# Five load tiles instead of three for the experts' weights, three instead of two for 64-bit input

## The chip, the cores and the metric

The kernel runs on one core of one Trainium2 chip. The core has five engines that each work through a queue of their own in order: TensorE (PE in the profile, with its weight loads as PEld), VectorE (DVE), ScalarE (ACT), GpSimd (POOL) and SyncE (SP), which here issues most of the DMAs. The metric is the device time of one execution in microseconds (us).

## What is computed

Three stages follow each other on the same data.

```python
X = np.fft.rfft(x, axis=1); y = np.fft.irfft(X * F, n=S, axis=1)        # (8, 3072, 256)
# mixture of experts on the 24576 rows, 8 experts, room for 768 rows each
h = np.maximum(np.einsum('ecd,edf->ecf', disp, w1), 0.0)                 # w1 (8, 256, 1024)
y = np.einsum('ecf,efd->ecd', h, w2)                                     # w2 (8, 1024, 256)
out[i] = gate_w[i] * y[expert_idx[i], pos[i]]                            # rows without a place stay zero
# then on all rows
return ((x @ w_a) * (x @ w_b)) @ w_out                                   # w_a, w_b (256, 1536), w_out (1536, 256)
```

The three matrices of the last stage arrive as 64-bit numbers.

## The kernel before

The program runs through a Fourier stage (to about 220 us), the experts' stage (to about 545 us) and the stage of the last three matrices (to the end). The change touches the experts' stage and what is done beside it.

**Steps.** The 8 experts have 768 places each, in 2 blocks of 384 rows: 16 blocks. A block is worked in 8 steps, one for each 128 of the 1024 hidden columns; `for s in range(nstep + 2)` counts 128 steps. In step s, `up` (L674) makes the hidden columns of one chunk with 6 matmuls, ACT and DVE split them into a high and a low half (`hh` L682, `hl` L683), and `down` (L686) adds the columns of step s-2 to the result with 6 matmuls. At a block's end ACT copies the result out (`yb`, L695) and stores it (L1155). In the fourth and fifth step of a block the rows of the next block are turned (L657 on PE, `xh` L658 on ACT, `xl` L659 on DVE), and in the seventh POOL fetches those of the block after it with three gathers (L646).

**Weights.** A chunk is 128 hidden columns of one expert, w1 and w2 together, 256 KB: 88 chunks, since experts 0 to 2 are loaded twice (their two blocks don't follow each other: the order is block 0 of experts 0, 1, 2, then block 1 of the same, then both blocks of 3 to 7). `load_chunk` (L618) gives each chunk a load on SP into a tile `raw` (two DMAs, L627 and L628) and a split: ACT copies it to `wh` (L633) and POOL subtracts to get `wl` (L634). The first 10 chunks have tiles of their own. From the 11th on the tiles `raw` are shared, a load waits until POOL has made `wl` of the chunk that had the tile, and a chunk is split in a fixed step, `at`, seven steps before its first use, and loaded in step `at - 3` of the program. While experts change with every block (steps 3 to 50) each step splits a chunk; later 8 of every 16 steps do.

**Conversion.** Beside this the 64-bit matrices are converted, 36 pieces, spread evenly over steps 17 to 119 (`convert`, L516; `moe2_steps`, L555). SP loads a piece into `raw64`; ACT squares its high words (`sq`, L533); DVE makes `ex` and `bits` (L534, L535), and half a piece later finishes (L541 to L544) into a tile `mix`, of which there are two. Two pieces make a factor of `w_a` or `w_b`: POOL makes four sums in `mix` (L579 to L582), ACT copies the high half (L564) and POOL subtracts the low half (L565, 2.1 us), after which `mix` is free. `ex` lies in PSUM, all else in SBUF.

**Zeros.** The rows of the output that no expert writes are filled from a tile of zeros by 48 DMAs on SP (L185), 18 of them in this stage. The tile `wide` holds zeros in its first half and the first rows of `w_out` in its second.

The order on each queue is the order in which the code is written; nothing is rescheduled.

Of the kernel before, what the change touches and what calls it, by code (L numbers as in the profile page):

```python
# [10 lines left out]
F32 = mybir.dt.float32  # L11
F32R = mybir.dt.float32r
# [9 lines left out]
P = 128  # L22
# [105 lines left out]
class Kernel:  # L128
# [48 lines left out]
            for k in range(4):  # L177
                nc.tensor.matmul(p[:, P * k:P * k + P], self.warm, self.warm, start=True, stop=True)

    def zero_steps(self, pool):  # L180

        v = self.io["out"].rearrange("(i p r) d -> i p r d", p=P, r=4)
        z = pool.tile([P, D], F32, name="zero")
        self.nc.vector.memset(z, 0.0)
        steps = [lambda i=i: self.nc.sync.dma_start(out=v[i], in_=bc(z[:, None, :], [P, 4, D]))  # L185
                 for i in range(NT // 512)]
        n = NB0 * S // 512
        return steps[:n], steps[n:]
# [327 lines left out]
    def convert(self, pc, src, to, pp=None):  # L516


        nc = self.nc
        v = nc.vector  # L520
        T = {}

        def load():
            T["raw"] = pc.tile([P, 256], I64, tag="raw64", name="raw64", bufs=2)
            nc.sync.dma_start(T["raw"], src)

        def make():
            w = T["raw"].bitcast(I32).rearrange("p (n t) -> p n t", t=2)
            lo, hi = w[:, :, 0].bitcast(U32), w[:, :, 1]
            ex = T["ex"] = (pp or pc).tile([P, 256], I32, tag="ex", name="ex", bufs=1)  # L530
            bits = T["bits"] = pc.tile([P, 256], I32, tag="bits", name="bits", bufs=1)
            sq = T["sq"] = pc.tile([P, 256], F32, tag="sq", name="sq", bufs=1)
            nc.scalar.activation(sq, hi.bitcast(F32), AF.Square)  # L533
            v.tensor_scalar(ex, hi, 3, 0x3FFFFFF8, ALU.logical_shift_left, ALU.bitwise_and)  # L534
            v.scalar_tensor_tensor(bits, hi, -0x40000000, ex, ALU.bitwise_and, ALU.bitwise_or)  # L535
            T["lo"] = lo

        def finish():
            bits, ex, sq, lo = T["bits"], T["ex"], T["sq"], T["lo"]
            f = ex.bitcast(F32)  # L540
            v.tensor_scalar(ex, bits, -0x800000, None, ALU.bitwise_and)  # L541
            v.scalar_tensor_tensor(f, lo, 2.0 ** -52, ex.bitcast(F32), ALU.mult, ALU.mult)
            v.tensor_tensor(f, f, bits.bitcast(F32), ALU.add)
            v.scalar_tensor_tensor(to(), sq.rearrange("p (a n) -> p a n", a=2), LEAST,  # L544
                                   f.rearrange("p (a n) -> p a n", a=2), ALU.is_ge, ALU.mult)

        return load, make, finish

    def moe2_tiles(self, pw):
        self.W = {n: (pw.tile([P, NU, 7, P], F32R, name=n + "h"), pw.tile([P, NU, 7, P], F32R, name=n + "l"))  # L550
                  for n in ("w_a", "w_b")}
        self.W["wide"] = pw.tile([P, 2 * D], F32R, name="wide")
        self.W["w_out"] = (pw.tile([P, 2 * DFF], F32R, name="w_outh"), pw.tile([P, 2 * DFF], F32R, name="w_outl"))

    def moe2_steps(self, pc, pp=None):  # L555


        nc, io = self.nc, self.io
        g = nc.gpsimd
        work = []  # L560

        def parts(src, dst):
            h, l = dst
            nc.scalar.copy(h, src)  # L564
            g.tensor_tensor(l, src, h.bitcast(F32), ALU.subtract)  # L565

        def factors(n, u):
            T = {}

            def c0():  # L570
                m = T["m"] = pc.tile([P, 8, P], F32, tag="mix", name="mix", bufs=2)
                return m[:, 0:8:7, :]

            def c1():
                return T["m"][:, 1:4:2, :]

            def mix():
                m = T["m"]
                g.tensor_tensor(m[:, 4], m[:, 7], m[:, 3], ALU.add)  # L579
                g.tensor_tensor(m[:, 5], m[:, 4], m[:, 0], ALU.subtract)  # L580
                g.tensor_tensor(m[:, 6], m[:, 0], m[:, 7], ALU.subtract)
                g.tensor_tensor(m[:, 2], m[:, 1], m[:, 5], ALU.subtract)  # L582

            src = io[n].rearrange("(c p) f -> p c f", p=P)[:, :, 256 * u:256 * u + 256]
            work.append(self.convert(pc, src[:, 0, :], c0, pp) + (None, None))
            work.append(self.convert(pc, src[:, 1, :], c1, pp) + (
                mix, lambda: parts(T["m"][:, 0:7, :], [t[:, u] for t in self.W[n]])))

        def plain(f):
            T = {}  # L590

            def to():
                T["o"] = pc.tile([P, 8, P], F32, tag="mix", name="mix", bufs=2)[:, 0:2, :]
                return T["o"]

            work.append(self.convert(pc, io["w_out"].rearrange("(c p) d -> p c d", p=P)[:, f, :], to, pp) + (
                None, lambda: parts(T["o"].rearrange("p a n -> p (a n)"),
                                    [t[:, f * D:f * D + D] for t in self.W["w_out"]])))

        def wide():  # L600
            nc.vector.memset(self.W["wide"][:, 0:D].bitcast(F32), 0.0)
            nc.vector.tensor_copy(self.W["wide"][:, D:], self.W["w_out"][0][:, 0:D].bitcast(F32))

        for u in range(NU):
            for n in ("w_a", "w_b"):
                factors(n, u)
        for f in range(DFF // P):
            plain(f)

        def step(i, stages):  # L610
            for k in stages:
                at = i - (0, 2, 2, 3, 4)[k]
                if 0 <= at < len(work) and work[at][k]:
                    work[at][k]()

        return [lambda i=i, k=k: step(i, k) for i in range(len(work) + 4) for k in ((1, 3), (2, 0, 4))] + [wide]

    def load_chunk(self, pa, e, f, pr=None, eng=None):  # L618
# [4 lines left out]
        T = {}  # L623

        def load():
            raw = T["raw"] = (pr or pa).tile([P, 4, P], F32, tag="raw", name="raw", bufs=NWC if pr else 3)
            nc.sync.dma_start(raw[:, 0:2, :], w1[:, P * f:P * f + P].rearrange("(c p) f -> p c f", p=P))  # L627
            nc.sync.dma_start(raw[:, 2:4, :].rearrange("p c d -> p (c d)"), w2[P * f:P * f + P, :])  # L628

# [40 lines left out]
    def ffn(self, pb, pp, w, x, y):  # L670
# [4 lines left out]
        def up(f):  # L675
            wh, wl = w[f]["h"], w[f]["l"]
            hp = self.ps()
            for c in range(2):
                self.mm3(hp[:, :BLK], wh[:, c, :], wl[:, c, :], x["h"][:, c, :], x["l"][:, c, :], c == 0, c == 1)
            hh = pb.tile([P, BLK], F32R, tag="hh", name="hh", bufs=4)  # L680
            hl = pb.tile([P, BLK], F32R, tag="hl", name="hl", bufs=4)
            nc.scalar.activation(hh, hp[:, :BLK], AF.Relu)  # L682
            nc.vector.scalar_tensor_tensor(hl, hp[:, :BLK], 0.0, hh.bitcast(F32), ALU.max, ALU.subtract)  # L683
            T[f] = (hh, hl)
# [240 lines left out]
def fast_path(K, outer):  # L925
# [4 lines left out]
    with ExitStack() as ctx:  # L930
# [177 lines left out]
        for c in range(NWC, 8 * len(turns)):  # L1108
            o = c - NWC
            at = (start[o // 8 + 1] - 1) * 8 + o % 8 + 3  # L1110
            ch = chunk(c)
            due.setdefault(at - 3, []).append(ch[0])
            due.setdefault(at, []).append(ch[1])
        conv, zero = [], []
        def load(k):
# [15 lines left out]
        for s in range(nstep + 2):  # L1131
# [6 lines left out]
            if s == 8 * NE - 9:  # L1138
# [4 lines left out]
                K.moe2_tiles(pw)  # L1143
                pc = pool("pc", "right", sC)
                conv = K.moe2_steps(pc, pp)
                zero, K.zeros = K.zero_steps(pw)
            if s < nstep:
                ups[k][s % 8]()
            for step in due.get(s, []):
# [143 lines left out]
```

## Time and profile before

| | |
|---|---|
| median of 3 runs | 1135.81 us (1134.91 to 1136.91) |
| profiled execution | 1140.07 us, of which the span of the core 1138.3 us |
| mean granted TensorE clock | 0.982 |
| busy in the span | PE 94%, PEld 90%, DVE 73%, POOL 59%, ACT 39% |

The profiled execution is 4.26 us above the median of the runs that were only timed. Matmuls overlap in the profile (one of 384 columns takes about 0.33 us and the next begins 0.17 us after it), so that a busy PE says less than the distance between the starts of its matmuls. A figure in brackets behind a row of the timeline is how long the engine was idle before it, and what ended that.

### The profile page before, as it was taken

Reading aid. Unit: us, or ns where it says so; the run is one execution under the profiler, and the core shown is the slowest. Engines: PE = TensorE matmul, PEld = TensorE weight load, DVE = VectorE, ACT = ScalarE, POOL = GpSimd, SP = SyncE. Lnnn points to the kernel's source line nnn. Section 1 sums busy time; section 2 is a strip of 40 time slices with the busy share of each in tenths; the row PEclk is TensorE's granted clock in tenths of the full one; section 3 lists DMA queues with packets and bytes.
Section 4 is the critical chain, followed back from the end, with each engine's and each line's share of the span. In section 5 each row is a group of like instructions: output and inputs, shape, how many; then the busy total and the mean of one; then the engine's idle time right before and its main releaser. Section 6 shows DMA issues by size and latency. Waiting matters only on the chain.

```text
span 1138.3 us, 19329 instructions
## 1 busy us (share of the span) xinstructions
PE 1075.0 (94%) x6908; PEld 1027.6 (90%) x6908; DVE 827.7 (73%) x1590; ACT 441.8 (39%) x894; POOL 673.9 (59%) x676
## 2 busy tenths in 40 slices
PE   7799998899998899999999999999999999999993
PEld 6777897869988899999899999999999999999993
DVE  2638788575456666673778888888888888888873
ACT  3564543454555555554332232332323223232220
POOL 1412645566788787653364765757657576575752
PEclk9999998989999999999999999999999999999997
DMA  9965824433667655662404004040040000100000
GB/s 222 192 210 178 258 71 140 122 133 127 196 221 216 200 175 180 205 201 78 153 1 138 30 1 149 20 139 29 1 149 20 29 28 1 38 19 1 29 1 31
DMA packets 109097, 123.27 MB, mean 108 GB/s; under 512 B 8576, under 2 KB 92544, under 8 KB 108992
## 3 DMA queue, kind: packets, MB, share of 16 engines
q1 hardware_dynamic: 93152, 87.34, 26.4%
q10 hardware_dynamic: 11232, 22.02, 5.3%
q0 software_dynamic: 4608, 12.59, 3.5%
q8 instruction: 56, 0.92, 0.3%
q14 instruction: 49, 0.40, 0.1%
HBM read 68.44 MB, written 53.48 MB: 107 GB/s over the span
## 4 chain that ended last, share of the span: by engine, by line
PE 72%; DMA 7%; issue 6%; POOL 5%; DVE 5%; SPq 2%; ACT 1%; POOLq 0%; DVEq 0%; ACTq 0%
PE ps L666 12%; PE ps L667 12%; PE ps L668 11%; PE po L831 6%; PE po L830 6%; PE po L829 5%; DMA raw<-w 3%; PE ps L374 3%; PE ps L333 3%; PE ps L310 3%; PE yp L667 2%; PE yp L668 2%; PE yp L666 2%; PE ps L391 2%; POOL wl L634 2%
## 5 line engine op out<-in xcount | busy, mean ns | idle before, releaser
L758 POOL TENSOR_TENSOR gl<-w_b,gh 128x384 fp32r<-128x384 f32 x190 | 194.3, 1034 | 196.0 <-ACT gh L757 195.8
L757 ACT CAST gh<-w_b 128x384 fp32r<-128x384 f32 x192 | 98.7, 514 | 262.2 <-DVE w_b L776 196.9
L830 PE MATMUL po<-w_outl,gh 128*128 128x256 f32 x576 | 160.9, 279 | 0.0
L831 PE MATMUL po<-w_outh,gl 128*128 128x256 f32 x576 | 160.6, 279 | 0.2 <-POOL gl L758 0.2
L829 PE MATMUL po<-w_outh,gh 128*128 128x256 f32 x552 | 154.0, 279 | 0.0
L634 POOL TENSOR_TENSOR wl<-raw,wh 128x512 fp32r<-128x512 f32 x88 | 112.6, 1291 | 52.9 <-ACT wh L633 30.1
L324 POOL TENSOR_TENSOR y<-t,t 112x512 f32<-112x512 f32 x48 | 65.7, 1368 | 129.8 <-DVE t L323 100.0
L683 DVE SCALAR_TENSOR_TENSOR hl<-ps,hh 128x384 fp32r<-128x384 f32 x128 | 70.5, 554 | 78.9 <-ACT hh L682 76.5
L666 PE MATMUL ps<-th,w_bh 128*128 128x384 f32 x336 | 114.7, 341 | 4.4 <-DVE w_a L769 4.4
L666 PE MATMUL ps<-th,w_ah 128*128 128x384 f32 x336 | 113.5, 338 | 1.2 <-DVE w_b L769 0.8
L667 PE MATMUL ps<-tl,w_ah 128*128 128x384 f32 x336 | 113.6, 338 | 1.1 <-DVE tl L723 0.5
L668 PE MATMUL ps<-th,w_al 128*128 128x384 f32 x336 | 113.2, 337 | 0.0
L667 PE MATMUL ps<-tl,w_bh 128*128 128x384 f32 x336 | 113.2, 337 | 0.0
L668 PE MATMUL ps<-th,w_bl 128*128 128x384 f32 x336 | 113.1, 337 | 0.0
L831 PEld LDWEIGHTS po<-w_outh,gl 128*128 128x128 f32 x576 | 108.1, 188 | 1.5 <-POOL gl L758 0.4
L830 PEld LDWEIGHTS po<-w_outl,gh 128*128 128x128 f32 x576 | 108.0, 187 | 0.0
L829 PEld LDWEIGHTS po<-w_outh,gh 128*128 128x128 f32 x552 | 103.6, 188 | 0.0
L666 PE MATMUL ps<-xh,wh 128*128 128x384 f32 x256 | 91.8, 359 | 5.8 <-DVE hl L683 5.2
L790 ACT COPY p<-ps 128x384 f32<-128x384 f32 x96 | 46.0, 479 | 127.4 <-PE ps L668 69.6
L776 POOL TENSOR_TENSOR w_b<-w_b,w_a 128x384 f32<-128x384 f32 x94 | 93.8, 1019 | 0.0
L682 ACT ACTIVATE hh<-ps 128x384 fp32r<-128x384 f32 x128 | 62.5, 488 | 74.1 <-PE ps L668 66.8
L666 PE MATMUL yp<-hh,wh 128*128 128x384 f32 x256 | 86.4, 337 | 4.9 <-ACT yb L695 4.7
(158 smaller groups left out, 2811.1 us busy)
## 6 DMA issues: line engine op xcount, KB each, us to landing
out<-zero SPq DMA_DIRECT2D x48, 512.0 KB
raw<-w SPq DMA_DIRECT2D x176, 128.0 KB
rows<-yt ACTq DMA_DIRECT2D x18, 512.0 KB
da<-sa ACTq DMA_DIRECT2D x12, 512.0 KB
sb<-da SPq DMA_DIRECT2D x32, 192.0 KB
yd<-yb ACTq DMA_DIRECT2D x16, 384.0 KB
y<-yd SPq DMA_DIRECT2D x8, 768.0 KB
sd<-x SPq DMA_DIRECT2D x12, 256.0 KB
```

The costliest lines, as they stand in the source:

```text
L324: eng.tensor_tensor(y, t1, t2, ALU.add)
L634: (eng or nc.gpsimd).tensor_tensor(l, T["raw"], h.bitcast(F32), ALU.subtract)
L666: mm(out, wh, xh, start=first, stop=False)
L667: mm(out, wh, xl, start=False, stop=False)
L668: mm(out, wl, xh, start=False, stop=last)
L683: nc.vector.scalar_tensor_tensor(hl, hp[:, :BLK], 0.0, hh.bitcast(F32), ALU.max, ALU.subtract)
L757: nc.scalar.copy(gh, g)
L758: (v if hurry and not ij[1] else nc.gpsimd).tensor_tensor(gl, g, gh.bitcast(F32), ALU.subtract)
L776: (v if hurry or ij in ON_V else nc.gpsimd).tensor_tensor(c, c, T["a"][ij], ALU.mult)
L829: mm(out, gh[:, sl], oh[:, o:o + D], start=False, stop=False)
L830: mm(out, gh[:, sl], ol[:, o:o + D], start=False, stop=False)
L831: mm(out, gl[:, sl], oh[:, o:o + D], start=False, stop=u == NU - 1 and i == 1 and j == 0)
```

## The change

`raw` gets five tiles and the loads stand one step earlier in the program; `raw64` gets three. Room is made in four places: `sq` moves from SBUF to PSUM, into one tile `two` with `ex`; the finishing steps leave their sum in `bits` (SBUF), where `ex` (PSUM) had it; `hh` and `hl` have three tiles each, not four; and the zeros are read from `wide`, whose first half is now cleared when the tile is made, so that the tile `zero` goes.

```diff
@@ zero_steps
-        z = pool.tile([P, D], F32, name="zero")
-        self.nc.vector.memset(z, 0.0)
+        z = wide[:, 0:D].bitcast(F32)
@@ convert
-            T["raw"] = pc.tile([P, 256], I64, tag="raw64", name="raw64", bufs=2)
+            T["raw"] = pc.tile([P, 256], I64, tag="raw64", name="raw64", bufs=3)
...
-            ex = T["ex"] = (pp or pc).tile([P, 256], I32, tag="ex", name="ex", bufs=1)
+            two = (pp or pc).tile([P, 2, 256], I32, tag="two", name="two", bufs=1)
+            ex, sq = T["ex"], T["sq"] = two[:, 0], two[:, 1].bitcast(F32)
             bits = T["bits"] = pc.tile([P, 256], I32, tag="bits", name="bits", bufs=1)
-            sq = T["sq"] = pc.tile([P, 256], F32, tag="sq", name="sq", bufs=1)
...
-            f = ex.bitcast(F32)
+            f = bits.bitcast(F32)
             v.tensor_scalar(ex, bits, -0x800000, None, ALU.bitwise_and)
-            v.scalar_tensor_tensor(f, lo, 2.0 ** -52, ex.bitcast(F32), ALU.mult, ALU.mult)
-            v.tensor_tensor(f, f, bits.bitcast(F32), ALU.add)
+            v.scalar_tensor_tensor(ex.bitcast(F32), lo, 2.0 ** -52, ex.bitcast(F32), ALU.mult, ALU.mult)
+            v.tensor_tensor(f, ex.bitcast(F32), f, ALU.add)
@@ moe2_tiles
         self.W["wide"] = pw.tile([P, 2 * D], F32R, name="wide")
+        self.nc.vector.memset(self.W["wide"][:, 0:D].bitcast(F32), 0.0)
@@ moe2_steps, wide
-            nc.vector.memset(self.W["wide"][:, 0:D].bitcast(F32), 0.0)
@@ load_chunk
-            raw = T["raw"] = (pr or pa).tile([P, 4, P], F32, tag="raw", name="raw", bufs=NWC if pr else 3)
+            raw = T["raw"] = (pr or pa).tile([P, 4, P], F32, tag="raw", name="raw", bufs=NWC if pr else 5)
@@ ffn, up
-            hh = pb.tile([P, BLK], F32R, tag="hh", name="hh", bufs=4)
-            hl = pb.tile([P, BLK], F32R, tag="hl", name="hl", bufs=4)
+            hh = pb.tile([P, BLK], F32R, tag="hh", name="hh", bufs=3)
+            hl = pb.tile([P, BLK], F32R, tag="hl", name="hl", bufs=3)
@@ fast_path
-            due.setdefault(at - 3, []).append(ch[0])
+            due.setdefault(max(0, at - 4), []).append(ch[0])
             due.setdefault(at, []).append(ch[1])
```

The order of the instructions on PE and POOL is the same in both programs. On SP the loads of weights move past the loads of 64-bit input and the zeros. This is SP's queue about step 22 before (the numbers are those of the program's tiles; `raw_3057` is one chunk's tile, `raw64_3039` one piece's):

```order
L525 DMA raw64_3039<-w_b 128x256 [waits DMAHW5_49,DVE_49]
L627 DMA raw_3057<-w1 128x2x128 [waits DMAHW6_49,DMAHW7_49,DMAHW0_49,Pool_49]
L628 DMA raw_3057<-w2 128x256
L627 DMA raw_3087<-w1 128x2x128 [waits DMAHW2_49,DMAHW1_49,Pool_49]
L628 DMA raw_3087<-w2 128x256
L525 DMA raw64_3103<-w_b 128x256 [waits DMAHW3_49,DVE_49]
L185 DMA out<-zero_2775 512x1x256 [waits DMAHW4_49]
L627 DMA raw_3121<-w1 128x2x128 [waits DMAHW5_49,Pool_49]
```

And the same place on SP in the changed program:

```order
L524 DMA raw64_3040<-w_b 128x256 [waits DMAHW7_49]
L627 DMA raw_3058<-w1 128x2x128 [waits DMAHW0_49,Pool_49]
L628 DMA raw_3058<-w2 128x256 [waits DMAHW1_49]
L627 DMA raw_3087<-w1 128x2x128 [waits DMAHW2_49,Pool_49]
L628 DMA raw_3087<-w2 128x256 [waits DMAHW3_49]
L524 DMA raw64_3103<-w_b 128x256 [waits DMAHW4_49,DVE_49]
L184 DMA out<-wide_2772 512x1x256 [waits DMAHW5_49]
L627 DMA raw_3121<-w1 128x2x128 [waits DMAHW7_49,Pool_49]
```

The sequence looks alike there, but each load of weights now stands one step ahead of the step that it belonged to, and its wait for POOL is for the subtraction of the chunk five before it in place of three; the second DMA of a chunk has got a wait for an earlier DMA on its semaphore (DMAHW).

On DVE the conversion of one piece, between the splits of the hidden columns (`hl`) and of turned rows (`xl`), stood like this before:

```order
L534 TENSOR_SCALAR ex<-raw_3039 128x256 [waits DMAHW5_49,DVE_49]
L535 SCALAR_TENSOR_TENSOR bits<-raw_3039,ex 128x256 [waits DVE_49]
L683 SCALAR_TENSOR_TENSOR hl<-ps,hh 128x384 [waits Activation_49]
L659 TENSOR_TENSOR xl<-ps,xh 128x384 [waits Activation_49]
L541 TENSOR_SCALAR ex<-bits 128x256 [waits DVE_49]
```

In the changed program the same five rows on DVE are:

```order
L534 TENSOR_SCALAR two<-raw_3040 128x256 [waits DMAHW7_49,Activation_49]
L535 SCALAR_TENSOR_TENSOR bits<-raw_3040,two 128x256 [waits DVE_49]
L683 SCALAR_TENSOR_TENSOR hl<-ps,hh 128x384 [waits Activation_49]
L659 TENSOR_TENSOR xl<-ps,xh 128x384 [waits Activation_49]
L541 TENSOR_SCALAR two<-bits 128x256 [waits DVE_49]
```

The first of them has got a wait for ACT: for the square of the same piece, which now writes into the same tile of PSUM.

On ACT, at the end of a block, copies and store stood like this before:

```order
L633 CAST wh<-raw 128x512 [waits DMAHW7_49,DMAHW6_49]
L695 COPY yb<-yp 128x384 [waits PE_49] x2
L1155 DMA yd_2008<-yb 128x768 [waits Activation_49]
L682 ACTIVATE hh<-ps 128x384 [waits PE_49]
L633 CAST wh<-raw 128x512 [waits DMAHW2_49,DMAHW1_49]
```

In the changed program this place on ACT reads:

```order
L633 CAST wh<-raw 128x512 [waits DMAHW7_49,DMAHW6_49]
L695 COPY yb<-yp 128x384 [waits PE_49] x2
L1155 DMA yd_2008<-yb 128x768 [waits DMAHW4_49,Activation_49]
L682 ACTIVATE hh<-ps 128x384 [waits DVE_49,PE_49]
L633 CAST wh<-raw 128x512 [waits DMAHW1_49,DMAHW0_49]
```

The store of a block's result has got a wait for an earlier DMA, here one of the loads of weights that were issued a few steps before, and `hh` one for DVE's reading of the tile's former content.

## Rows read from the trace of the kernel before

**Rows 1.** Page, 40 slices of the span, busy tenths of PE and POOL.
```profile
PE   7799998899998899999999999999999999999993
POOL 1412645566788787653364765757657576575752
```

**Rows 2.** Stretches: us, busy time of each engine, granted clock, DMA share, GB/s.
```profile
301.30:383.37 82.07, 72.92 (x410) 68.85 (x410) 49.32 (x115) 45.12 (x95) 69.94 (x71) 1.00 0.67 210
340.00:360.00 20.00, 16.98 (x97) 16.10 (x97) 12.64 (x30) 11.62 (x25) 19.07 (x21) 1.00 0.69 211
383.37:400.68 17.31, 17.31 (x104) 17.24 (x103) 13.83 (x34) 10.40 (x21) 11.57 (x13) 1.00 0.74 229
```

**Rows 3.** Timeline of PE: first matmul of steps 23, 55, 63, 71, 79 and 87.
```profile
301.30 0.33 PE L666 MATMUL ps<-xh,wh 128*128 128x384 f32 x1
...
383.37 0.33 PE L666 MATMUL ps<-xh,wh 128*128 128x384 f32 x1
...
400.68 0.33 PE L666 MATMUL ps<-xh,wh 128*128 128x384 f32 x1
...
419.82 0.33 PE L666 MATMUL ps<-xh,wh 128*128 128x384 f32 x1
...
437.14 0.33 PE L666 MATMUL ps<-xh,wh 128*128 128x384 f32 x1
...
455.27 0.33 PE L666 MATMUL ps<-xh,wh 128*128 128x384 f32 x1
```

**Rows 4.** Waits from 301.30 to 383.37: us in total, times, longest us.
```profile
ACT wh L633 <- DMA raw<-w: 30.7, 18, 5.0
DVE hl L683 <- ACT hh L682: 23.1, 11, 4.2
POOL wl L634 <- ACT wh L633: 9.7, 9, 2.0
...
DVE mix L544 <- POOL w_bl L565: 2.8, 1, 2.8
```

**Rows 5.** Waits of SP's DMA queue from 283 to 384 us.
```profile
SPq L627 <- POOL wl L634: 35.5, 23, 5.0
...
SPq L525 <- DVE ex L542: 7.1, 2, 3.7
```

**Rows 6.** Timeline: one weight tile's way through POOL, SP and ACT to PE.
```profile
345.39 1.30 POOL L634 TENSOR_TENSOR wl<-raw,wh 128x512 fp32r<-128x512 f32 x1
346.72 0.38 SPq L627 DMA_DIRECT2D raw<-w  x1
347.14 0.81 SPq L628 DMA_DIRECT2D raw<-w  x1
350.77 0.62 ACT L633 CAST wh<-raw 128x512 fp32r<-128x512 f32 x1 [2.71 <-DMA raw<-w]
351.82 0.45 PE L666 MATMUL yp<-hh,wh 128*128 128x384 f32 x1 [2.79 <-ACT yb L695]
```

**Rows 7.** Timeline of ACT, in the blocks from 400.68 and 437.14.
```profile
413.06 0.62 ACT L633 CAST wh<-raw 128x512 fp32r<-128x512 f32 x1 [3.67 <-DMA raw<-w]
...
449.35 0.63 ACT L633 CAST wh<-raw 128x512 fp32r<-128x512 f32 x1 [3.16 <-DMA raw<-w]
```

**Rows 8.** Groups of POOL from 301.30 to 383.37: busy, mean ns, idle before.
```profile
L646 POOL DMA_INDIRECT rowt<-rows,gidx x12 | 12.0, 1003 | 3.0 <-issue 2.1 <-PE yp L668 0.3
```

**Rows 9.** Timeline of DVE: two finishing instructions that waited for POOL.
```profile
372.11 0.42 DVE L544 SCALAR_TENSOR_TENSOR mix<-sq,ex 128x256 f32<-128x256 f32 x1 [2.79 <-POOL w_bl L565]
...
478.82 0.42 DVE L544 SCALAR_TENSOR_TENSOR mix<-sq,ex 128x256 f32<-128x256 f32 x1 [4.30 <-POOL w_outl L565]
```

**Rows 10.** Timeline of DVE and ACT: first instructions of one 64-bit piece.
```profile
366.54 0.42 DVE L534 TENSOR_SCALAR ex<-raw 128x256 int32<-128x256 int32 x1
...
366.65 0.43 ACT L533 ACTIVATE sq<-raw 128x256 f32<-128x256 f32 x1
```

**Rows 11.** Timeline: clearing of `zero` on DVE, last store of rows on ACT.
```profile
284.21 0.27 DVE L184 MEMSET zero<- 128x256 f32 x1
...
259.96 0.40 ACTq L395 DMA_DIRECT2D rows<-yt  x1
```

More of the change, by code (lines that the diff above doesn't have):

```diff
@@ L178, in warm_up, with zero_steps @@
                 nc.tensor.matmul(p[:, P * k:P * k + P], self.warm, self.warm, start=True, stop=True)
-    def zero_steps(self, pool):
+    def zero_steps(self, wide):
         v = self.io["out"].rearrange("(i p r) d -> i p r d", p=P, r=4)
-        z = pool.tile([P, D], F32, name="zero")
-        self.nc.vector.memset(z, 0.0)
+        z = wide[:, 0:D].bitcast(F32)
         steps = [lambda i=i: self.nc.sync.dma_start(out=v[i], in_=bc(z[:, None, :], [P, 4, D]))
@@ L1145, in fast_path @@
                 conv = K.moe2_steps(pc, pp)
-                zero, K.zeros = K.zero_steps(pw)
+                zero, K.zeros = K.zero_steps(K.W["wide"])
             if s < nstep:
```

## The prediction

> **What bounds the kernel now.** I began with the page's slices [rows 1]: PE is busy at eight or nine tenths almost everywhere, and POOL at seven to eight tenths from the eleventh slice to the sixteenth (a slice is 28.5 us), some 285 to 455 us. In the first part of that stretch each step of the experts' stage splits a chunk, so the two engines are compared there.
>
> The starts of PE's first matmul of a step give the length of each block [rows 3]. The block 383.37 to 400.68 takes 17.31 us, and its stretch shows PE busy for all of it [rows 2]: that is what 8 steps cost when nothing is late. The four blocks from 301.30 to 383.37 take 82.07 us where 4 x 17.31 = 69.24 would do, so **12.83 us** are lost. Later blocks lose less: 400.68 to 419.82 is 19.14 (1.83 lost), 437.14 to 455.27 is 18.13 (0.82 lost). The granted clock is 1.00 in all of these stretches, which is the 2.4 GHz level, so the loss is waiting and not a lower clock.
>
> Next, who waits for what there [rows 4]. The largest line is ACT, 30.7 us in 18 waits of the copy `wh` for `raw`, up to 5.0 each. Second is DVE's `hl` for ACT's `hh`, 23.1 us: a consequence, since `hh` stands behind `wh` in ACT's queue. SP's queue tells why `raw` is late [rows 5]: 23 loads waited 35.5 us for POOL's `wl`. The reader can follow one turn of this circle in the timeline [rows 6]: POOL ends `wl` at 346.69, the load is issued 0.03 us later, its second half at 347.14 for 0.81, ACT starts the copy only at 350.77 after 2.71 us of idling, then copies `yb`, and PE has stood still 2.79 us for that `yb` when it starts at 351.82. ACT's queue is worked in order, so the late copy holds back `yb` though PE has its result ready. The same wait appears once each in the later lossy blocks: 3.67 at 413.06 and 3.16 at 449.35 [rows 7].
>
> So PE pays for a transfer that begins only when POOL has finished. But POOL itself is nearly full. In the four blocks it is busy 69.94 us [rows 2], and its 12 gathers have 3.0 us before them in which it issues [rows 8]: 72.9 us of work it can't avoid, which is more than PE's 69.24. Between 340 and 360 us it is busy 19.07 of 20, with three gathers' issuing (2.1 x 3/12 = 0.5) 98%.
>
> **The change part by part.**
>
> *Five tiles, loads a step earlier.* A load now waits for the `wl` of the chunk five before. Two more chunks are two steps, at least 2 x 17.31/8 = 4.3 us of lead, against waits of 1.7 us on average (30.7/18) and 5.0 at most: nearly every wait of `wh` for `raw` should go. What comes back is not the whole 12.83. ACT and PE can then run ahead only as far as POOL follows: `wl` is still made chunk by chunk, and POOL must do 72.9 us of work. Lower bound of the gain: POOL reaches no more than the 98% that it already shows: 72.9/0.98 = 74.4, gain 82.07 - 74.4 = **7.7**. With POOL never idle it is 9.2; if POOL's work could be caught up in the blocks after it (in 383.37 to 400.68 it is busy only 11.57 of 17.31) and PE never waited, 12.83. I take 7.7, since POOL's row is the nearest to a bound: its split of a chunk is due seven steps ahead, which is some slack, but five tiles still tie loads, and the two `mix` tiles tie DVE, to where POOL stands.
>
> For the later blocks: at 413.06 the load of that chunk waited likewise for a `wl` that stood behind POOL's backlog; with two chunks more the backlog no longer reaches the load, and I count the whole 1.83. For 437.14 to 455.27 I count half, 0.4, because a block with turned rows and 64-bit pieces has other small waits (bounds 0 and 0.82). Other blocks gain nothing: one of them loses 1.9 us to DVE's wait of 4.30 at 478.82 for POOL's `w_outl` [rows 9], which no tile of `raw` touches.
>
> *Three tiles for 64-bit input.* SP's loads of 64-bit pieces waited 7.1 us for DVE between 283 and 384 [rows 5], and a load of weights behind them on the same queue waits with them. With three tiles they wait for the finish of the piece three before, which lies further back. Gain beside the first part: nothing, as loads of weights will be early anyway. Without it, the loads would be held up to 3.7 us, inside the 4.3 us of lead.
>
> *`sq` in PSUM with `ex`.* The number of instructions is the same. DVE's first instruction of a piece now waits for ACT's square. In the trace DVE began it at 366.54, and ACT the square at 366.65 for 0.43 [rows 10]: it would slip about 0.5 us. Behind it in DVE's queue stand the rest of the piece and the next `hl`; but that `hl` waits for `hh`, which stands behind the square on ACT anyway. So the cost is mostly covered: bounds 0 and 36 pieces x 0.5 = 18 us if each slip reached PE. I take 0.01 per piece, about 0.3 us, nearest to the row of `hl`, which waits for ACT 23.1 us in these blocks already.
>
> *`hh` and `hl` with three tiles.* A tile is read by `down` two steps after its making, and PE does that `down` before the next `up`, by program order. So PE can't want a fourth. `hh` now waits for DVE's reading of a tile written three steps ago: over 6 us back. Cost 0; if DVE lagged three steps behind, PE would already stand.
>
> *The store of a block's result* on ACT now also waits for an earlier load on the same semaphore. That load is one that a coming `wh` needs anyway. While loads are early it costs nothing; if late, `hh` behind it waits as it did before. I take 0.2 us over all blocks, bounds 0 and one load's 2.7 [rows 6].
>
> *The zeros from `wide`.* One clearing of 0.27 us on DVE goes and another moves from the conversion to the making of the tile [rows 11]. The clearing must wait for the stores of rows that read the same room; the last was issued at 259.96, 24 us ahead of 284.21. Cost 0, cover 24 us.
>
> **Sum:** 7.7 + 1.8 + 0.4 - 0.3 - 0.2 = **9.4 us**. Nothing after 545 us changes but its start. The profiled execution of 1140.07 would become 1130.7; it lies 4.26 above the median, and that stays, so the median goes from 1135.81 to **1126.4**.
>
> The Trainium skill ("Perfetto Trace Analysis", Identifying the Most-Contended Engine) says to improve the engine with the highest occupancy, and to judge TensorE by its weight loads, not by its matmuls. By that rule POOL is the engine between 340 and 360 (19.07, weight loads 16.10 of 20 [rows 2]), and the change takes no work off it. The trace bears the rule out in so far as every late load begins 0.03 us after POOL's `wl`; by it the four blocks could give at most POOL's idle time, 82.07 - 72.9 = 9.2, where the waits alone would give 12.83.
>
> **The rivals.** A measurement of this kernel tells about 0.2% (2.3 us) from no change.
>
> *A, the forecast:* POOL bounds the four blocks, 6 to 13 us come back, chance 0.62.
>
> *B, the backlog comes out elsewhere.* ACT and DVE no longer held by `raw`, the conversion runs into its two `mix` tiles: DVE's last finishing instruction waits for POOL's part, as it does at 372.11 for 2.79 and at 478.82 for 4.30 [rows 9], and `hl` stands behind it. The four blocks are 32 of the 103 steps over which 36 pieces are spread, so some 11 pieces or 5 to 6 factors fall into them; at 0.5 to 1 us more each, 3 to 6 us of the 9.4 are lost again. Gain 2.3 to 6, about 1132. For it: POOL's rows. Against it: only one such wait is in the four blocks, 2.8 us [rows 4]. Chance 0.18.
>
> *C, no change.* Either the loads are late by the transfer itself (the DMA share is 0.67 there [rows 2], and if more loads in flight only share the same engines, landing slips by as much as issue gains), or POOL's whole backlog eats the gain. Against it: in the undisturbed block the DMA share is higher, 0.74, and nothing waits. Time 1134 to 1138. Chance 0.11.
>
> *D, slower.* The square stands behind a `wh` in ACT's queue; DVE's first instruction waits through that, with `xl` and `hl` behind it. It decides the sign when the 36 pieces cost more than (9.4 + 2.3)/36 = 0.33 us each on PE's path. At the 0.5 us of slip all uncovered it is 18 us against 9.7 gained, 1144. Against it: the cover named above; DVE is busy 49.32 of 82.07 [rows 2]. Chance 0.06.
>
> The Trainium skill ("PSUM — Partial Sum Buffer", PSUM bank collisions raise a hardware error) says that ScalarE and VectorE must be kept from one bank of PSUM at the same time whatever the addresses. The order of the changed program agrees: the new wait stands where `sq` and `ex` share a tile; no run here shows what would happen without it.
>
> *E, more than forecast.* POOL catches up behind the blocks and PE loses nothing: 12.83 + 1.83 + 0.82 = 15.5, so 1120.3. Against it: POOL's 72.9 beside PE's 69.24. Chance 0.03 for more than 13.
>
> **How the numbers follow.** The time is A's. Its own range, 6 to 13 us, is 1122.8 to 1129.8 with chance 0.62; to hold 8 in 10 the range must take in most of B, up to 1132.5 (a gain of 3.3), and below it reaches E's bound, 1120.5. Left out are C, D and the weak end of B, about 0.2. Faster by over 0.2%: A, B and E, 0.83. Same: C, 0.11. Slower: D, 0.06.
>
> **What would show it.** Right: between 301 and 383 the waits of `wh` for `raw` fall from 30.7 to under 5 us; PE's four blocks take 73 to 76 us; POOL is busy over 93% of them; the waits of the SP queue for `wl` may stay, but are no longer followed by an idle ACT; the idling at 413.06 and 449.35 is gone; a block without splits still takes 17.31. B shows as longer waits of `mix` L544 for POOL's parts and of `hl` behind them; C as `wh` waiting for `raw` as before with loads issued earlier; D as waits of `two` L534 for ACT, with PE waiting for `hl`. The prediction is wrong if the four blocks take over 79 or under 70 us, or if the time moves outside the experts' stage.

## The result and the profile after

The changed kernel takes **1126.36 us** (median of 5 runs, 1124.34 to 1128.39), before 1135.81 in the same comparison: ratio 0.9918, 95% interval 0.9897 to 0.9939. That is faster by more than the 0.2% named in the prediction.

The two profiled executions differ by more, 1138.3 and 1122.5 us of span, and this has to be cleared up first. From the first matmul of step 7 (260.41 before, 253.97 after) to that of step 127 (543.22 and 527.40) the change saves 282.81 - 273.43 = **9.38 us**; behind step 127 both spans have 595.1 us left. The other 6.4 us lie ahead of step 7, where the granted clock between 210 and 240 us was 0.90 in the one execution and 1.00 in the other. In the twelve experiments step 0 began between 225.1 and 231.1 us, and steps 0 to 7 took between 25.2 and 29.9 us, whatever was changed, so these 6.4 us are taken as the execution's, not the kernel's. From here on kernels are compared over steps 7 to 127. Each kernel has one profiled execution, so a difference of a microsecond or so between two stretches is a hint and no more.

PE's first matmuls of steps 23, 31, 39, 47 and 55 in the timeline of the changed kernel (start, duration) answer to [rows 3]:

```profile
294.87 0.33 PE L666 MATMUL ps<-xh,wh 128*128 128x384 f32 x1
312.20 0.33 PE L666 MATMUL ps<-xh,wh 128*128 128x384 f32 x1
329.53 0.33 PE L666 MATMUL ps<-xh,wh 128*128 128x384 f32 x1
348.75 0.33 PE L666 MATMUL ps<-xh,wh 128*128 128x384 f32 x1
369.24 0.33 PE L666 MATMUL ps<-xh,wh 128*128 128x384 f32 x1
```

The four blocks take 74.37 us in place of 82.07, where 74.4 were forecast. But they aren't alike: 17.33, 17.33, 19.22 and 20.49. Two lose nothing, two lose 5.1 us together. The stretches of the changed kernel, all four blocks, the first two and the last two (us, busy time of each engine, clock, DMA share, GB/s), answer to [rows 2]:

```profile
294.87:369.24 74.37, 70.50 (x410) 69.00 (x409) 51.33 (x118) 45.38 (x95) 68.63 (x69) 1.00 0.75 228
294.87:329.53 34.66, 34.66 (x206) 34.53 (x206) 25.51 (x58) 23.18 (x50) 30.79 (x31) 1.00 0.75 232
329.53:369.24 39.71, 35.84 (x206) 34.47 (x205) 25.82 (x61) 22.20 (x46) 37.84 (x39) 1.00 0.74 224
```

POOL (the fifth pair) is busy 89% of the first two blocks and 95% of the last two. The waits in the four blocks, which answer to [rows 4]:

```profile
ACT hh L682 <- PE ps L668: 14.4, 20, 1.6
DVE hl L683 <- ACT hh L682: 6.9, 8, 1.5
...
DVE mix L544 <- POOL w_bl L566: 4.8, 1, 4.8
...
PEld ps L657 <- DMA rowt<-rows,gidx: 3.1, 4, 1.5
...
DVE two L534 <- ACT two L533: 1.6, 6, 0.4
```

ACT's largest wait is now for PE, the engine that should end last, and the line of `wh` waiting for `raw`, 30.7 us before, is gone. SP's queue from 276 to 370 us, which answers to [rows 5]:

```profile
SPq L627 <- POOL wl L634: 30.3, 24, 5.0
SPq L524 <- DVE two L542: 8.5, 1, 8.5
```

The loads wait for POOL nearly as long as before, 30.3 us against 35.5, but ACT no longer waits behind them. For instance the chunk loaded at 330.10 in the changed kernel is copied at 335.37, without idle time of ACT before it, 3.5 us after SP was done with its second half (330.73 + 1.09).

What PE still loses is mostly in two places (a third, 0.5 us at 362.47, is again for rows). In the timeline of PE, two starts in the last two blocks (idle before, and what ended it):

```profile
341.96 0.33 PE L657 MATMUL ps<-ident,rowt 128*128 128x128 f32 x1 [1.30 <-DMA rowt<-rows,gidx]
...
360.20 0.44 PE L667 MATMUL yp<-hl,wh 128*128 128x384 f32 x1 [1.76 <-DVE hl L683]
```

And what DVE and POOL did ahead of the second:

```profile
359.26 0.42 DVE L544 SCALAR_TENSOR_TENSOR mix<-two,bits 128x256 f32<-128x256 f32 x1 [4.80 <-POOL w_bl L566]
```
```profile
348.29 5.05 POOL L634 TENSOR_TENSOR wl<-raw,wh 128x512 fp32r<-128x512 f32 x4
353.48 1.01 POOL L646 DMA_INDIRECT rowt<-rows,gidx  x1
354.79 1.00 POOL L646 DMA_INDIRECT rowt<-rows,gidx  x1 [0.30 <-issue]
356.10 1.00 POOL L646 DMA_INDIRECT rowt<-rows,gidx  x1 [0.30 <-issue]
357.12 2.11 POOL L566 TENSOR_TENSOR w_bl<-mix,w_bh 128x896 fp32r<-128x896 f32 x1
```

Four subtractions and three gathers stand ahead of `w_bl` in POOL's queue; until it ends, DVE gets no tile `mix`, and `hl` stands behind DVE's wait. The late gathers hold PE the other way, through the turned rows.

### The profile page after: what moved, and what is told of

Read it like the earlier page. It is cut to its first block, busy times and chain, and to the rows that moved or that the text cites. A ratio compares the mean times of both kernels' runs of the same rounds, so it can differ in the third digit from the quotient of the medians.

```text
span 1122.5 us, 19362 instructions
## 1 busy us (share of the span) xinstructions
PE 1068.8 (95%) x6908; PEld 1023.9 (91%) x6908; DVE 828.7 (74%) x1589; ACT 442.6 (39%) x894; POOL 673.9 (60%) x676
## 4 chain that ended last, share of the span: by engine, by line
PE 80%; DMA 6%; DVE 4%; issue 4%; POOL 2%; SPq 1%; ACT 1%; ACTq 0%; DVEq 0%; POOLq 0%
PE ps L666 13%; PE ps L667 13%; PE ps L668 13%; PE po L831 6%; PE po L830 6%; PE po L829 5%; PE yp L667 3%; PE yp L668 3%; PE yp L666 3%; PE ps L373 3%; PE ps L332 3%; PE ps L309 3%; PE ps L390 2%; PE ps L264 2%; DMA fr<-fr 1%
## 5 line engine op out<-in xcount | busy, mean ns | idle before, releaser
L667 PE MATMUL yp<-hl,wh 128*128 128x384 f32 x256 | 86.0, 336 | 3.9 <-DVE hl L683 3.9
```

The lines of the kernel that those rows point to most:

```text
L667: mm(out, wh, xl, start=False, stop=False)
```

## The experiments

All were timed in five rounds against the kernel before, whose medians there were 1135.47 us (e1 to e4), 1135.40 (e5 to e8) and 1135.19 (e9 to e12); the ratios go by these. The four blocks are steps 23 to 55, as in the prediction; both stretches are distances between PE's first matmuls of a step, read from the timeline of the profiled execution.

| kernel | median us | ratio (95%) | four blocks | steps 7 to 127 |
|---|---|---|---|---|
| before | 1135.81 | | 82.07 | 282.81 |
| changed | 1126.36 | 0.9918 (0.9897 to 0.9939) | 74.37 | 273.43 |
| e1 tiles only | 1127.29 | 0.9925 (0.9895 to 0.9954) | 74.81 | 273.89 |
| e2 all but the tiles | 1138.28 | 1.0026 (1.0002 to 1.0050) | 83.95 | 284.86 |
| e3 four tiles | 1127.28 | 0.9916 (0.9887 to 0.9946) | 74.55 | 273.58 |
| e4 `w_out` first | 1122.65 | 0.9876 (0.9844 to 0.9908) | 74.85 | 271.30 |
| e5 three `mix` | 1122.81 | 0.9891 (0.9862 to 0.9919) | 73.40 | 269.53 |
| e6 both | 1119.04 | 0.9865 (0.9836 to 0.9894) | 69.48 | 266.56 |
| e7 rows earlier | 1124.72 | 0.9902 (0.9873 to 0.9931) | 72.21 | 271.96 |
| e8 before, `w_out` first | 1133.43 | 0.9986 (0.9970 to 1.0002) | 81.40 | 280.67 |
| e9 e2, square in SBUF | 1141.37 | 1.0056 (1.0035 to 1.0078) | 82.96 | 289.63 |
| e10 before, three `mix` | 1135.43 | 0.9986 (0.9965 to 1.0006) | 82.03 | 280.55 |
| e11 before, both | 1132.04 | 0.9965 (0.9946 to 0.9985) | 75.65 | 275.71 |
| e12 e6, rows earlier | 1120.72 | 0.9866 (0.9836 to 0.9896) | 70.23 | 267.65 |

**Which part of the change did it?** e1 makes one part alone, from the kernel before:

```diff
-tag="raw", name="raw", bufs=NWC if pr else 3
+tag="raw", name="raw", bufs=NWC if pr else 5
-due.setdefault(at - 3, []).append(ch[0])
+due.setdefault(max(0, at - 4), []).append(ch[0])
-tag="hh", name="hh", bufs=4
+tag="hh", name="hh", bufs=3
-tag="hl", name="hl", bufs=4
+tag="hl", name="hl", bufs=3
```

> The kernel before with only the five tiles for weights and their load one step earlier, and hh and hl with three tiles to make room; 64-bit input keeps two tiles, sq and the zeros stay where they were. Theory (the late loads of weights were the whole gain, the other parts cost and bring nothing): about the time of the full change, 1126.4 us, ratio 0.990 to 0.994, the four blocks of steps 23 to 55 in 74 to 75 us. Rival (the third tile for 64-bit input is needed, since loads of weights stand behind held 64-bit loads on SP): half of the gain or less, 1130 to 1133 us, four blocks 77 to 80 us, with wh waiting for raw again.

It gives the whole gain. The 64-bit loads were held on SP for 16.3 us around the four blocks (up to 9.5) and the loads of weights stood behind them, yet `wh` waited for `raw` only 1.6 us there, in two waits, and none of PE's waits in these blocks is for them. The rival falls. What e1 doesn't separate is the two extra tiles from the earlier place of the load. No run has the earlier place with three tiles. Before the change 23 loads already stood at the head of SP's queue and waited for POOL, which an earlier place alone would not have ended; that is an argument, not a measurement.

e2 is the changed kernel with three tiles and their load three steps ahead again:

```diff
-tag="raw", name="raw", bufs=NWC if pr else 5
+tag="raw", name="raw", bufs=NWC if pr else 3
-due.setdefault(max(0, at - 4), []).append(ch[0])
+due.setdefault(at - 3, []).append(ch[0])
```

> The changed kernel with the weights' tiles back at three and their loads back at three steps ahead; all else as changed. Theory: no change against before, 1134 to 1138 us, four blocks 81 to 83 us, wh waiting for raw about 30 us in them. If the new waits (square in PSUM, store of a block's result) cost what was put down, 0.5 us, that can't be seen. Rival (sq in PSUM costs DVE, or 64-bit input brings something by itself): over 1139 or under 1132 us.

None of the gain is left; if anything it is slower, the interval just clears 1. Two waits of its four blocks, and one turn of them in the timelines of ACT and DVE:

```profile
ACT wh L633 <- DMA raw<-w: 28.3, 15, 5.3
DVE two L534 <- ACT two L533: 13.2, 7, 4.5
```
```profile
374.59 0.62 ACT L633 CAST wh<-raw 128x512 fp32r<-128x512 f32 x1 [5.28 <-DMA raw<-w]
375.11 0.39 ACT L533 ACTIVATE two<-raw 128x256 f32<-128x256 f32 x1
...
375.54 0.43 DVE L534 TENSOR_SCALAR two<-raw 128x256 int32<-128x256 int32 x1 [4.50 <-ACT two L533]
```

This is rival D's wait, real as soon as `wh` is late: the square stands behind `wh` on ACT, and DVE behind the square. In the changed kernel the same line is 1.6 us. So the tiles also remove the condition under which the square's place costs. Whether it is the cause of e2's 0.26% was to be settled by e9, which puts `sq` back into a tile of its own in SBUF:

```diff
-            two = (pp or pc).tile([P, 2, 256], I32, tag="two", name="two", bufs=1)
-            ex, sq = T["ex"], T["sq"] = two[:, 0], two[:, 1].bitcast(F32)
+            ex = T["ex"] = (pp or pc).tile([P, 256], I32, tag="ex", name="ex", bufs=1)
+            sq = T["sq"] = pc.tile([P, 256], F32, tag="sq", name="sq", bufs=1)
```

> e2 (three tiles for weights, all other parts of the change) with sq back in SBUF, so that DVE's first instruction of a piece no longer waits for ACT's square. In e2 these waits were 13.2 us in the four blocks, up to 4.5 each, where the square stood behind a copy wh that waited for raw. Theory (that wait is what made e2 slower than before): 1135 to 1136 us, four blocks 81 to 83 us. Rival (e2's excess is chance, or comes from the stores and zeros): 1138 us again, four blocks 83 to 84.

The wait went and the four blocks came out as the theory had them, but the kernel got slower still (the block of steps 95 to 103 takes 22.60 us, 19.20 before), for a reason that neither theory had: the finishing instruction L544 now reads `sq` and `bits`, both in SBUF, and its mean in the four blocks went from 0.42 us to

```profile
L544 DVE SCALAR_TENSOR_TENSOR mix<-sq,bits 128x256 f32<-128x256 f32 x12 | 21.2, 1769 | 3.3 <-POOL w_bl L566 2.7
```

(the last section shows why). So e9 doesn't settle e2's excess, and that stays open. In e2's profiled four blocks 19 pairs of matmuls start 0.32 us apart in place of 0.17, at a lower granted clock; that is 2.9 us, more than the 1.9 by which these blocks exceed those of before, and would do by itself for this one execution; whether it does for the median of 12 runs isn't known.

**How many tiles?** e3 has four, from the changed kernel:

```diff
-tag="raw", name="raw", bufs=NWC if pr else 5
+tag="raw", name="raw", bufs=NWC if pr else 4
```

> The changed kernel with four tiles for weights in place of five, loads still four steps ahead. One tile is one step, 2.16 us, of lead; of the waits of before about a third were longer. Theory: wh waits for raw a few times more, 1 to 3 us each, four blocks 75 to 77 us, 1127 to 1129 us. Rival (POOL's work alone sets the four blocks once loads don't wait for the chunk three before): the same as with five tiles, 74.4 and 1126.4 us.

The same time as with five. `wh` waits for `raw` again, 6.0 us in 5 waits, none over 1.7, as the theory had it; yet the blocks are no longer, as the rival had it. PE itself waited in these blocks for nothing but turned rows (2.8 us), so the waits of `wh` didn't reach it.

**Is POOL's work what is left?** e4 takes some of it out of the four blocks, from the changed kernel:

```diff
-        for u in range(NU):
-            for n in ("w_a", "w_b"):
-                factors(n, u)
         for f in range(DFF // P):
             plain(f)
+        for u in range(NU):
+            for n in ("w_a", "w_b"):
+                factors(n, u)
```

> The changed kernel, converting the 12 pieces of w_out first and the 24 pieces of w_a and w_b after them (two loops swapped). A piece of w_out costs POOL 0.74 us, a piece of w_a or w_b (4 x 0.46 + 2.12)/2 = 1.98, and 11 pieces fall into the four blocks: POOL has some 14 us less to do there, about 59 of 69. Theory (POOL's work is what is left of the loss there): all four blocks at 17.3 to 17.5 us, 69 to 70 in all, 5 us less; some 1121 to 1123 us. Rival (the two mix tiles bind DVE, whatever POOL's load, and a piece of w_out takes a tile for itself): DVE's last finishing instruction waits more often, the four blocks stay at 73 to 77 us, 1126 us or above.

Here the theory fell in the four blocks, and with it a good part of my reasoning. POOL is busy 11 us less, and the blocks are not shorter:

```profile
294.40:369.25 74.85, 70.18 (x409) 68.89 (x409) 50.66 (x117) 44.34 (x101) 57.84 (x53) 1.00 0.73 224
...
DVE mix L544 <- POOL w_outl L566: 15.0, 6, 4.6
```

DVE's waits for a tile `mix` have taken the place. One of them, in the timelines of POOL and DVE:

```profile
313.47 1.01 POOL L646 DMA_INDIRECT rowt<-rows,gidx  x1
314.79 1.00 POOL L646 DMA_INDIRECT rowt<-rows,gidx  x1 [0.30 <-DMA raw<-w_out]
316.09 0.99 POOL L646 DMA_INDIRECT rowt<-rows,gidx  x1 [0.30 <-issue]
317.10 0.74 POOL L566 TENSOR_TENSOR w_outl<-mix,w_outh 128x256 fp32r<-128x256 f32 x1
...
317.88 0.42 DVE L544 SCALAR_TENSOR_TENSOR mix<-two,bits 128x256 f32<-128x256 f32 x1 [4.20 <-POOL w_outl L566]
```

POOL is not short of time here; three gathers take 3.6 us of its queue at once, and a part of 0.74 us behind them is all that DVE waits for. What e4 gains, 2.1 us over steps 7 to 127, comes from the blocks of steps 87 to 103, 34.97 in place of 37.39 us. So its time lies in the theory's range, but not for the theory's reason.

e5 gives `mix` a third tile, in both places where one is made, its 4 KB a partition from one tile of `raw` and one of `raw64`:

```diff
-tag="mix", name="mix", bufs=2
+tag="mix", name="mix", bufs=3
-bufs=NWC if pr else 5
+bufs=NWC if pr else 4
-tag="raw64", name="raw64", bufs=3
+tag="raw64", name="raw64", bufs=2
```

> The changed kernel with three tiles mix in place of two; the room for it from one tile for weights (four) and one for 64-bit input (two), neither of which cost time in the earlier runs. In the profile of the changed kernel PE loses 2.1 us behind hl at 358.11, where DVE waited 4.8 us for POOL's w_bl, and 2.9 more in the blocks of steps 87 to 103 in the same way; another 3 us are lost to rows fetched late by POOL. Theory (after the change the two mix tiles bind, DVE waits in its queue for POOL's parts): the first 5 us come back, the rows stay late: four blocks at about 72, steps 87 to 103 at 34.7 in place of 37.4, some 1122 us. Rival (POOL's work is all that counts in the four blocks): these stay at 74 to 75 and only the later blocks gain, 1124 us.

DVE's waits for `mix` are gone (no line of it is left), and the blocks of steps 87 to 103 take 34.65 us, as forecast. But the four blocks gain 1.0 and not 2.4: the third and fourth are 19.77 and 19.00, now all by rows that POOL fetched late (1.77 and 1.19 us between two turns). The rival was nearer there.

e6 is e5 with the loops of e4.

> The same with three mix tiles, and the pieces of w_out converted first as in e4. Theory (two limits in series: POOL's work, which e4 took away, and the two mix tiles, which hid that): all four blocks at 17.3 to 17.6, 69.3 to 70.5 in all, later blocks without loss too, some 1117 to 1119 us. Rival (in e4 the waits of DVE came from POOL's gathers, which take 3.9 us of the queue at once, and one tile more is not enough): 72 to 75 in the four blocks, 1121 us.

This is the theory's number for the four blocks, where only 0.2 us are lost; in the later blocks 0.9 us stay lost, in steps 95 to 103.

```profile
295.86:365.34 69.48, 69.48 (x410) 69.01 (x409) 51.15 (x117) 43.85 (x101) 57.45 (x53) 1.00 0.77 239
```

e4 gains 0 there, e5 1.0, both together 4.9: two limits in series, each of which hides what the other costs. This holds for the four blocks alone. In the blocks behind them each remedy by itself takes away what is lost in steps 87 to 103, so over steps 7 to 127 the two gain 2.1 and 3.9 us alone and 6.9 together, and by the medians 3.7 and 3.6 alone and 7.3 together: over the whole kernel hardly more than their sum. e6 is the best version found, 16.3 us under before over steps 7 to 127; its interval overlaps those of e4 and e5, but not that of the changed kernel.

e7 issues the gathers one step earlier in the changed kernel:

```diff
-if s % 8 == 6 and NE <= k + 2 < len(order):
+if s % 8 == 5 and NE <= k + 2 < len(order):
```

> The changed kernel with the three gathers of a block issued one step earlier (sixth step of a block in place of the seventh). Theory (rows come late because the gathers stand behind POOL's backlog; one step is 2.16 us): PE's waits for turned rows, 1.7 us at 340.33 and 0.9 at 361.60, go, four blocks at about 72, some 1124 us. Rival (POOL's work is the bound, so that what the gathers gain the parts lose): another wait takes their place, four blocks 74 to 75, 1126 us.

The four blocks are 72.21, PE no longer waits for rows there, and the theory holds for the stretch. Steps 95 to 103 gain 0.95 as well, but a new loss of 1.6 us in the block of steps 111 to 119 (19.12 after 17.51) takes half of the sum back. The time, 1124.72, can't be told from the changed kernel's. e12 does the same in e6:

> e6 with the gathers of a block one step earlier. What e6 has left over 17.32 us a block between steps 23 and 119 is 1.1 us, 0.9 of it in the block of steps 95 to 103. Theory: at most that comes back, which the times can't tell from e6: 1118 to 1120 us. Rival (the gathers run into another piece of POOL's work, as a wait of 1.8 us did in e7's block of steps 111 to 119): 1120 to 1122 us.

Nothing is gained: 267.65 against 266.56.

**What ended last before the change?** The same remedies on the kernel before, with its three tiles: e8 is e4's edit, e10 the third `mix` with three tiles of `hh` and `hl` for its room, e11 both. Of e10:

```diff
-tag="mix", name="mix", bufs=2
+tag="mix", name="mix", bufs=3
-tag="hh", name="hh", bufs=4
+tag="hh", name="hh", bufs=3
-tag="hl", name="hl", bufs=4
+tag="hl", name="hl", bufs=3
```

> The kernel before, three tiles for weights, with the pieces of w_out converted first. Theory (loads were late only because POOL's subtraction was behind, and 14 us less work for POOL brings the loads in time even with three tiles): waits of wh for raw in the four blocks under 10 us in place of 30.7, blocks limited by the two mix tiles as in e4, 75 to 77 us, 1125 to 1129 us in all. Rival (three tiles are too few whatever POOL does, as a gather or a part holds the queue for 3 to 4 us and each load waits behind it): waits of 15 us and more, four blocks 79 us or above, 1130 us or above.

> The kernel before with hh and hl at three tiles and mix at three in place of two, weights still with three tiles. Theory (of the limits in series the late loads end last; the mix tiles show only when these are gone): the four blocks gain at most the 2.8 us of DVE's one wait there, 79 to 82 us, later blocks 2 us, 1132 to 1135 us. Rival (DVE's ties to POOL were the cause and the loads a consequence): under 1130 us, four blocks under 78.

> The same with the pieces of w_out converted first, still three tiles for weights. e6 with four tiles took 69.48 us for the four blocks. Theory (three tiles are too few even when POOL has slack, since a load waits behind any gather or part that POOL has ahead of the subtraction; e8 had 11.9 us of such waits): four blocks 72 to 76 us, 1122 to 1126 us. Rival (with POOL's work and the mix tiles mended three tiles are enough): four blocks under 71 us, 1119 us as in e6.

Alone, neither moves the time measurably. e8 missed its theory: `wh` waits for `raw` 11.9 us and not under 10, DVE 16.2 for `mix`, and the blocks are at 81.40, some 3 us of it in two spells of a lower clock behind stalls of PE (last section). Its rival, which wanted waits of 15 us and more, isn't met either. e10 came out at the upper end of its theory (82.03 and 1135.43). In e11, with slack on POOL and one wait for `mix` of 1.6 us left, `wh` still waits 19.7 us for `raw` in 13 waits, and the four blocks take 75.65; the time, 1132.0, is above the 1122 to 1126 expected, though its profiled stretch saves 7.1 us; that execution took 1128.71, among the fastest of its 12, so the stretch may flatter it. So three tiles were too few by themselves, and not only because POOL was behind.

## Why the prediction was right, point by point

- **The circle of late loads** is what the change broke. Waits of `wh` for `raw` went from 30.7 us to none that the view lists, and e1 shows that the tiles and the earlier load, together, do it without the other parts. Not every late load began 0.03 us after POOL, as the prediction has it: of the 18 copies that waited in the four blocks before, 14 had such a load, and the other four had one issued 0.3 to 1.2 us after POOL's last subtraction. e11 adds that the circle needs no shortage of POOL's time: one gather or part ahead of the subtraction is enough.
- **The term 7.7** measured 82.07 - 74.37 = 7.70. Its mechanism, POOL at 98% over all four blocks, is only half right. POOL was busy 68.63 of 74.37, which is 92% and just under the 93% named as a sign, and 96% with the 3.0 us of issuing; two blocks ran free and two were held. And e4 showed that less work for POOL alone brings nothing there, because the two `mix` tiles, which the prediction had as rival B, hold DVE to the same length. The size agrees; that it would come out of POOL's busy time to 0.1 us was luck. The working shows it too: 72.9 counts 3.0 us of idling before the gathers as work, the 98% only 2.1. With 3.0 in both the share is 99% and the term 8.5. The better statement is that POOL's queue is the limit by its order as well as its load: what stands behind gathers and subtractions comes late. The bound of 9.2 from POOL's idle time held for the change, but it is no firm bound: e7, which takes no work off POOL, has the four blocks in 72.21, a gain of 9.86. POOL was busy 67.19 us in them and 12.76 in the block behind, where before it was 69.94 and 11.57, so a part of its work can be made up later. The Trainium skill ("Perfetto Trace Analysis", Identifying the Most-Contended Engine) says to optimise the engine with the highest occupancy first. These runs agree only in part: to take 11 us of work off POOL brought nothing in these blocks by itself (e4), and with a third `mix` both together brought 4.9 us (e6).
- **The later blocks.** Steps 63 to 71: 17.31, the whole 1.83 as forecast. Steps 79 to 87: 17.33, 0.80 gained where half of it, 0.4, was put down. Steps 87 to 95: 18.19 after 17.37, a loss of 0.8 that the sum didn't have; DVE waited 3.19 us for `w_bl` at 443.74, rival B in small. The two errors, 0.4 too little and 0.8 too much, partly cancel. Steps 95 to 103 stayed at 19.20, as said. That the median met the forecast within 0.1 us is more than the working earned: the runs alone spread over 4 us.
- **The third tile for 64-bit input** brought nothing, as said (e1 without it has the same time), and for the reason said, since the loads of weights are early anyway. But the hold was put too low, at 3.7 us: it was up to 9.5 in e1, and with the third tile still 8.5 at once in the changed kernel.
- **`sq` in PSUM** cost DVE 1.6 us of waiting in the four blocks and 4.7 in all, in 10 waits; PE's two losses named above stand behind other waits. The 0.3 us forecast on the path can't be told from 0. With three tiles for weights the wait is 13.2 us (e2): the cover that the prediction counted on holds only while `wh` is early.
- **The store's new wait** did happen once in the four blocks, and ACT was held 1.72 us (timeline of ACT in the changed kernel):

```profile
335.88 0.86 ACT L695 COPY yb<-yp 128x384 f32<-128x384 f32 x2
338.09 0.33 ACTq L1155 DMA_DIRECT2D yd<-yb  x1
338.46 0.95 ACT L565 CAST w_ah<-mix 128x896 fp32r<-128x896 f32 x1 [1.72 <-DMA raw<-w]
```

  PE had no gap up to 339.93, and the one behind that is for rows, so the store's wait was covered; its bound had been 2.7.
- **Zeros, `hh` and `hl`**: the clearing of `wide` ran at 277.8 and waited for nothing; e2 shows that no part beside the tiles and their earlier load brings a gain.

## What to carry to other kernels

When a wait is removed, look for the next one in the queue of the engine that released it: here one in-order queue (POOL) released loads, rows and conversion tiles, and each remedy alone ran into the next tie. In the four blocks two remedies that each brought little (0 and 1.0 us) brought 4.9 together, so such remedies have to be tried together; over the whole kernel their gains did little more than add up. And a limit that is read from an engine's busy time says nothing of the order in its queue: a part of 0.74 us behind three gathers held DVE for 4.2.

## What the runs showed of the hardware

**DVE and POOL on SBUF.** In e9 L544 reads two operands in SBUF; in the kernels before and after one of its two is in PSUM, 0.42 us each. In e9 one such instruction took 7.18 us (timeline of DVE, then of POOL):

```profile
345.04 7.18 DVE L544 SCALAR_TENSOR_TENSOR mix<-sq,bits 128x256 f32<-128x256 f32 x1
```
```profile
344.89 3.76 POOL L634 TENSOR_TENSOR wl<-raw,wh 128x512 fp32r<-128x512 f32 x3
348.61 2.11 POOL L566 TENSOR_TENSOR w_al<-mix,w_ah 128x896 fp32r<-128x896 f32 x1
350.68 1.26 POOL L634 TENSOR_TENSOR wl<-raw,wh 128x512 fp32r<-128x512 f32 x1
352.30 0.46 POOL L580 TENSOR_TENSOR mix<-mix 128x128 f32<-128x128 f32 x1 [0.37 <-DVE mix L544]
```

It began 0.15 us after POOL's first of five subtractions and ended 0.3 us behind the fifth, when POOL, for the first time, had to wait itself. Where POOL is between instructions or in a gather, L544 takes 0.42 in e9 too (at 360.88). The Trainium skill ("SBUF — State Buffer", Who interferes with whom) says that DVE and GpSimd share a port pair, that this pair is an exclusive lock, and that a DVE instruction with two inputs in SBUF contends with a GpSimd instruction that reads SBUF. The trace agrees: L544 took 0.42 us beside a gather and mostly longer beside POOL's subtractions, 1.77 on average in the four blocks. In the case shown DVE didn't get in between POOL's five instructions, which followed each other without a gap. That isn't always so, as another place of e9 shows (timelines of DVE and POOL):

```profile
406.20 0.62 DVE L544 SCALAR_TENSOR_TENSOR mix<-sq,bits 128x256 f32<-128x256 f32 x1
...
405.25 2.72 POOL L634 TENSOR_TENSOR wl<-raw,wh 128x512 fp32r<-128x512 f32 x2
```

L544 was done at 406.82, in the course of POOL's two subtractions, which took 2.72 us together where two took 2.57 at 358.42. What decides between the two cases stays open. The shared port would explain why the changed kernel, which moves the sum into `bits`, does well to move `sq` to PSUM; no run has the changed kernel's five tiles with both in SBUF.

**The clock after a stall of PE.** In e8 PE stood still for 3.27 us up to 323.26. Behind it the matmuls start 0.32 us apart in place of 0.17, and the granted clock (third from the end of a row) is 0.50, the lower level of 1.2 GHz:

```profile
320.00:324.00 4.00, 0.74 (x3) 0.74 (x4) 1.69 (x4) 1.85 (x4) 3.68 (x5) 0.96 0.63 216
324.00:327.00 3.00, 3.00 (x11) 3.00 (x11) 2.09 (x6) 1.49 (x5) 2.65 (x3) 0.50 0.72 221
```

About ten matmuls at 0.15 us more each are 1.5 us on top of the stall. It isn't tied to the length of one stall alone. Between the starts of two matmuls e8's stall is 3.61 us; the execution shown of before kept a clock of 1.00 behind one of 3.12 (348.69 to 351.82), while e1 had such a spell behind one of 2.73, and e3 had one (0.51 from 347.30 to 350.50) with no stall over 1.52 ahead of it. What decides it stays open here. It makes the four blocks of e1, e2, e3, e8 and e10 in their profiled executions longer by 1 to 3 us than their waits alone.
